# Two queries' attends side by side on TensorE, and the eight PSUM banks shared out anew for the query stage

## The chip, the cores and the metric

One core of one Trainium2 chip runs the whole program. The metric is the device time of one execution in microseconds (us). Of several runs the median is given; a profile comes from one execution, and its span leaves out what lies ahead of the first and behind the last instruction.

Engines are named as the profile names them: PE is TensorE's matmul side and PEld its weight load, DVE is VectorE, ACT is ScalarE, POOL is GpSimd, SP is SyncE, which here issues transfers and loads registers. PSUM is the memory that PE writes to; it has eight banks of 128 partitions by 512 fp32 values.

## The reference, cut to what matters

```python
q, k, v = split(x @ wqkv)                       # 2048 tokens, 16 heads of 28
phi_q = concat(softmax(q @ w_phi), softmax(-(q @ w_phi)))     # 56 features a head; phi_k likewise
num = phi_q @ (phi_k^T @ v)                     # linear attention, per head
den = phi_q @ sum(phi_k) + 1e-6
a = (num / den) @ wo
# top 2 of 8 experts for each token, gated
b = sum over the two experts e of w_e * (silu(x @ w1[e]) @ w2[e])
out = sigmoid(x . gate_w) * a + (1 - that) * b
```

The change touches only the query side of the attention: phi_q, num, den and the product with wo.

## The kernel before, in words

The 2048 tokens are 16 tiles of 128; t counts them. The kernel runs in three stages, one after the other on PE: first values and keys of all tiles, then the queries, then the experts. The order of PE, ACT, DVE and (around the query stage) POOL is the order in which the code is written: each engine does its instructions in turn, and a wait holds up all that stands behind it on that engine.

The query stage is the loop `for t in range(NT + 2)` (L1175). For one query tile the work goes through these steps, which lie in different passes of the loop:

- `ask(t)` (L635): eleven products `pq<-WHq,WLq` on PE into one bank of tag A. `signs` (L573) copies them and their negative into an `eq` buffer on ACT, `tops` (L579) takes maxima on DVE, `drop` (L584) subtracts them on POOL (`eq<-eq,mxq`, L586), `raise_` (L644) takes the exponential on ACT (L645).
- `flip(t)` (L706): eight transposes `et<-ident,eq` on PE in two halves of four, each half into a bank of tag O, each copied out by ACT (L713). It is called two passes ahead of the attend.
- `attend(t)` (L880): 32 matmuls `n<-B,et` with 64 by 64 tiles of the array into a pair of banks of tag T. The trace shows two records for each.
- `weigh(t, n_)` (L888): six DVE instructions that read `n` (L895 to L901), then two on POOL that make `om` (L906, L908).
- `turn(t)` (L910), one pass later: four transposes `ot<-ident,om` into a bank of tag O, and `xsplit` (L136), a copy on ACT (`oh<-ot`, L137) and two subtractions on DVE (L139, L140), which read that bank last.
- `project(t)` (L918), one pass later still: eleven products `ao` into tag A, left by ACT in `leave_row` (L923) and written out by SP.

One pass of the loop thus holds, on PE in this order: attend(t), flip(t+2), project(t-2), turn(t-1), ask(t+7), and in the late passes the transposes `xgt` of `first_tokens` (L851), a turn of gathered rows for the experts, into tag O and read by ACT (L824) and DVE (L828, L829). On POOL: up to three stores `tabd<-rec` of `store` (L473), which wait for the matmul in `behind`, here the attend of the pass; then `drop`, then `om`. In pass 0 or 1 `route` (L397) lets PE count the experts' tokens into a bank `pp` of tag O, which DVE reads at L458, behind `xsplit` of query 0.

The banks are shared out once for the whole program: two for A (L91, `BANKS`), four for O, one pair for T (L94). A tile of a tag gets a bank when the last reader of the tile that held it is done.

The functions that the diff touches, and what calls them:

Of the kernel before, what the change touches and what calls it, by code (L numbers as in the profile page):

```python
# [8 lines left out]
F32 = mybir.dt.float32  # L9
# [6 lines left out]
PSUM = bass.MemoryType.PSUM  # L16
DRAM = bass.MemoryType.DRAM

P = 128
# [6 lines left out]
NT = S // P  # L26
# [25 lines left out]
QASKS = {t: t + 7 for t in range(9)}  # L52
# [10 lines left out]
LANDING = ("x00", "w0", "x10", "x20", "x30", "w1", "x01", "x40", "x11", "x50", "x21", "w2", "x31", "w3", "x41", "x51")  # L63
PIECES = ("00", "10", "20", "30", "01", "40", "11", "50", "21", "02", "12", "22", "31", "41", "03", "13", "23",
          "32", "51", "42", "52", "33", "43", "53")
BANKS = {"A": 2, "O": 4}
XLP = range(3, 16)
QBUFS = 5
ASKS = {9: 0, 10: 1, 11: 2, 12: 3, 14: 4}
# [2 lines left out]
NJ = 8  # L72
# [10 lines left out]
def gated_mix(ctx: ExitStack, tc: tile.TileContext, xt, xq, wk, wq, wv, wphi, wo, w12, out):  # L83
# [3 lines left out]
    cst = ctx.enter_context(tc.tile_pool(name="cst", bufs=1))  # L87
    dram = ctx.enter_context(tc.tile_pool(name="dram", bufs=1, space=DRAM))
    ps = ctx.enter_context(tc.tile_pool(name="ps", bufs=1, space=PSUM))

    def bank(tag, name):  # L91
        return ps.tile([P, 512], F32, tag=tag, name=name, bufs=BANKS[tag])

    def two_banks(name):  # L94
        return ps.tile([P, NJ, P], F32, tag="T", name=name, bufs=1)

    def after(i, others):
        for o in others:
# [21 lines left out]
    reached = {}  # L120
# [15 lines left out]
    def xsplit(xh, xl, src, eng):  # L136
        nc.scalar.activation(xh, src, AF.Copy)  # L137
        lo = xh[64:P, 3]
        for i in (eng.tensor_tensor(out=lo, in0=src[64:P, 3], in1=lo.bitcast(F32), op=ALU.subtract),  # L139
                  eng.tensor_tensor(out=xl, in0=src[:, 0:3], in1=xh[:, 0:3].bitcast(F32), op=ALU.subtract)):  # L140
            if eng is nc.gpsimd:
                in_turn(i)
# [21 lines left out]
    pe = pe_stack.enter_context(tc.tile_pool(name="pe", bufs=1, side="right"))  # L164
# [63 lines left out]
    for what in LANDING:  # L228
        t = int(what[1])
# [41 lines left out]
    for t in range(NT):  # L271
        pool = pe if t < NT // 2 else px
# [3 lines left out]
    for n, m in (("k", D), ("v", VG), ("q", D), ("o", D)):  # L276
        pool = px if n in "qo" else pb
# [75 lines left out]
    for what in LANDING:  # L353
        t = int(what[1])
# [3 lines left out]
        c = FIRST[int(what[2])]  # L358
# [114 lines left out]
    def store(n, behind=()):  # L473
        for at, what in stores[:n]:
            i = in_turn(nc.gpsimd.indirect_dma_start(
                out=tabd[:, :], out_offset=bass.IndirectOffsetOnAxis(ap=at, axis=0), in_=what, in_offset=None), "slots")
            after(i, [*filled, *behind])
            for o in sc:
                tc.declare_no_dep(i.ins, o.ins, reason="slots of their own")
            sc.append(i)  # L480
        del stores[:n]
# [91 lines left out]
    def signs(e, src):  # L573
        e4 = signed(e)
        nc.scalar.activation(e4[:, :, 0], src, AF.Copy)
        nc.scalar.activation(e4[:, :, 1], src, AF.Copy, scale=-1.0)


    def tops(e, n, pool):  # L579
        mx = pool.tile([P, H, 2], F32, tag="mx", name=f"mx{n}", bufs=2)  # L580
        nc.vector.tensor_reduce(out=mx, in_=signed(e), axis=AX.X, op=ALU.max)
        return mx

    def drop(e, mx):  # L584
        e4 = signed(e)
        in_turn(nc.gpsimd.tensor_tensor(out=e4, in0=e4, in1=mx.unsqueeze(3).to_broadcast([P, H, 2, DH]),  # L586
                                        op=ALU.subtract))

    def lower(e, n, pool):
        drop(e, tops(e, n, pool))  # L590
# [36 lines left out]
    def advance(n):  # L627
        for _ in range(n):
            if routes and next(routes[0], 0) == 0:
                del routes[0]  # L630
# [13 lines left out]
    def raise_(t):  # L644
        nc.scalar.activation(EQ[t][:, :, 0:56], EQ[t][:, :, 0:56], AF.Exp)  # L645
# [19 lines left out]
    for t in range(NT):  # L665
# [19 lines left out]
        if 1 <= t < 5:  # L685
            c = t - 1
# [193 lines left out]
    def attend(t):  # L880
        n_ = two_banks(f"n{t}").rearrange("p (a j) (b d) -> p a (j b) d", a=2, b=2)
        for j in range(NJ):
            for a, h in enumerate(half):
                for b in half:
                    reached["n"] = nc.tensor.matmul(n_[b, a, j, 0:60], et[t][h, j, b], B[h, j], start=True, stop=True)
        return n_.rearrange("p a j d -> p (a j) d")
# [20 lines left out]
                                        in0=w5[:, :, :, 0], in1=w5[:, :, :, 1], op=ALU.add))  # L907
        in_turn(nc.gpsimd.tensor_copy(o[:, D:512], o[:, 384:D]))  # L908

    def turn(t):  # L910
        oh[t] = pc.tile([P, 4, P], F32R, tag="oh", name=f"oh{t}")
        ol[t] = pc.tile([P, 3, P], F32R, tag="ol", name=f"ol{t}")
        tp = bank("O", f"ot{t}").rearrange("p (c n) -> p c n", n=P)
        for c in range(4):
            nc.tensor.transpose(tp[:, c], om[t][:, c * P:(c + 1) * P], ident)
        xsplit(oh[t], ol[t], tp, nc.vector)
# [11 lines left out]
    def table():  # L928
        for r in range(E):
            v = nc.values_load(byrank[0:1, r:r + 1], engines=SPONLY, min_val=0, max_val=E - 1)  # L930
            todo = [(tabm[:, r * nm:(r + 1) * nm], tabd[bass.ds(v * OWN, MAIN), :], P)]
            if r < LARGE:
                n = extra(r)
                for h in range(copies(r)):
                    todo.append((tabx[h * n:(h + 1) * n, r:r + 1], tabd[bass.ds(v * OWN + MAIN, n), :], n))
            for dst, src, p in todo:
                i = nc.sync.dma_start(dst, src.rearrange("(c p) two -> p c two", p=p))
                after(i, sc)

    def rows(lo, hi):  # L940
        in_turn(nc.gpsimd.tensor_scalar(idm[:, lo * nm:hi * nm], tabm.bitcast(I32)[:, lo * nm:hi * nm, 0], float(S - 1), None,
                                op0=ALU.min))
        if lo < LARGE:
            hi = min(hi, LARGE)
            in_turn(nc.gpsimd.tensor_scalar(idx[:, lo:hi], tabx.bitcast(I32)[0:EX, lo:hi, 0], float(S - 1), None, op0=ALU.min))
# [218 lines left out]
    def fill_in():  # L1164
        n = len(fill)
        fill.append((*FILL[n // 2], n % 2))
        first(*fill[-1])

    def part_way():
        for g in list(coming):  # L1170
            if next(g, 0) == 0:
                coming.remove(g)

    at, k = None, 0
    for t in range(NT + 2):  # L1175
        u = t + QAHEAD
        if t - 1 in QASKS:
            signs(EQ[QASKS[t - 1]], pq[QASKS[t - 1]])
        elif t == 0:
            signs(EQ[6], pq[6])  # L1180
        if 1 <= t and u - 1 < NT:
            raise_(u - 1)
        advance(QSTEPS.get(t, 2))
        early_top = u < NT and t < LOWER
        if early_top:
            top = tops(EQ[u], f"q{u}", pr)
        if at is not None and t == at + 1:
            store(LASTS, behind)
            table()
        if t < NT:  # L1190
            n_ = attend(t)
        behind = [reached["n"]]
        store(STORES.get(t, 3) if at is None or at == NT else 0, behind)
        if at is None and not routes:
            routes.append(ranks())
            at = NT
        if at == NT and len(stores) <= LASTS and not routes:
            at = t
        k = t - (NT if at is None else at)
        if k == ROWS + 1:  # L1200
            rows(0, 1)
        for c in ASKED.get(k - ROWS, ()):
            gather(0, c, behind)
        if early_top:
            drop(EQ[u], top)
        if t < NT:
            weigh(t, n_)
        if u < NT and not early_top:
            lower(EQ[u], f"q{u}", pr)
        if t + 2 < NT:  # L1210
            flip(t + 2)
        if t >= 2:
            if t == NT + 1:
                fill_in()
            leave_row(t - 2, project(t - 2))
        if t == NT:
            fill_in()
        if 1 <= t <= NT:
            turn(t - 1)
        if t in QASKS:  # L1220
            ask(QASKS[t], some=(0 if t else 5, 11))
        if t == NT - 1:
            fill_in()
        if t == PEND:
            pe_stack.close()
            pm = ctx.enter_context(tc.tile_pool(name="pm", bufs=2, side="right", reuse_waits="tile"))
            pw = ctx.enter_context(tc.tile_pool(name="pw", bufs=1, side="right", reuse_waits="tile"))
            ph = ctx.enter_context(tc.tile_pool(name="ph", bufs=2, side="right", reuse_waits="tile"))
        if k == ROWS + 3:
            rows(1, E)  # L1230
        if k == 2:
            load(0)
            splits += [halve(0, 1), halve(0, 2)]
        part_way()
        if ROWS + 2 <= k < ROWS + 3 + nm:
            g = first_tokens(k - ROWS - 2)
            next(g)
            coming.append(g)
        if SPLIT <= t < SPLIT + 3 and splits:
            if next(splits[0], 0) == 0:  # L1240
                del splits[0]
                if splits:
                    next(splits[0])
    assert not coming and not splits
    runs["on"] = False
    pc_stack.close()
    px_stack.close()
# [14 lines left out]
    for s in range(E * NFC):  # L1262
# [28 lines left out]
        n = 3 * nm  # L1291
        if e == E - 1 and fc > NFC - LATE:
            n = n // 2 if fc < NFC - 1 else 0
        if fc % 2 == 0:
            f = first_pair(e, fc // 2)
# [7 lines left out]
    with tc.manual_schedule(engines={mybir.EngineType.PE}):  # L1303
        last = reached["pe"]
        for cs in ((0, 1), (2,), (3,)):
            for at in (0, 2):
                for c in cs:
                    for i in range(2):
                        share(E - 1, NFC - LATE + at + i, c, last)
                    if at:  # L1310
                        leave(E - 1, (c,))
    pf_stack.close()


    loads, (n_ov,) = nc.values_load_multi_w_load_instructions(nov_i[0:1, 0:1], min_val=0, max_val=MAXOV)  # L1315
# [98 lines left out]
```

## Time and profile before

| what | value |
|---|---|
| median of 3 runs | 790.08 us (789.95 to 791.45) |
| the profiled execution's own time | 790.2 us |
| its span | 788.2 us |
| PE busy | 777.1 us, 99% of the span |
| DVE, ACT, POOL busy | 483.4, 308.9, 339.9 us |
| granted TensorE clock, mean | 0.998 |

The profiled execution lies 0.1 us above the median, and 2.0 us of its time lie outside the span. A row of the timeline gives the start, the time from the first start to the last end of the records that it merges, the engine, the line, the operation with what it writes and reads, how many records, and in brackets how long the engine sat idle before and what released it. Matmuls overlap: one that is listed with 0.37 us lets the next start after about 0.20 us, so differences of starts tell what PE spends on a group.

### The profile page before, as it was taken

The page shows a single profiled execution, that of the slowest core. Times are in us where ns is not written, and L with a number is a line of the kernel's source. Part 1 is how long each engine was busy: PE and PEld are TensorE (multiplying, and loading weights), DVE is VectorE, ACT ScalarE, POOL GpSimd, SP SyncE. Part 2 cuts the span into 40 slices and gives each one's busy share as a digit, 9 for nine tenths or more (in the row PEclk, how much of TensorE's full clock was granted, in tenths as well). Part 3 has the DMA queues.
Part 4 walks back from the last instruction along what each step waited for, and adds up shares of the span by engine and source line. Part 5 has one row for each costly group of instructions (what it writes and reads, how often), then busy time and mean ns, then how long its engine had stood idle before and what let it go on. Part 6 is the DMA issues. An engine that isn't in the chain of part 4 may idle for free. (4 is left out here: it accounts for less than half of the span.)

```text
span 788.2 us, 18163 instructions
## 1 busy us (share of the span) xinstructions
PE 777.1 (99%) x7378; PEld 721.4 (92%) x7378; DVE 483.4 (61%) x1045; ACT 308.9 (39%) x523; POOL 339.9 (43%) x334
## 2 busy tenths in 40 slices
PE   8999999999999999999999999999999999999996
PEld 6888888989999999998999799999999999999995
DVE  4698978658684866574566345554754555475431
ACT  5543455556532433343334223333433333243221
POOL 4667878886223316423450147144325405423003
PEclk9999999999999999999999999999999999999999
DMA  8420000135253337324543264364345336435403
GB/s 280 121 86 1 2 2 26 38 54 180 98 170 90 111 105 164 127 94 97 144 139 109 63 144 147 112 154 130 123 120 153 129 125 157 137 129 115 134 2 46
DMA packets 39786, 85.92 MB, mean 109 GB/s; under 512 B 11312, under 2 KB 20928, under 8 KB 39700
## 3 DMA queue, kind: packets, MB, share of 16 engines
q1 hardware_dynamic: 29332, 67.88, 26.3%
q0 software_dynamic: 10224, 16.61, 11.3%
q8 instruction: 59, 0.97, 0.5%
q10 hardware_dynamic: 144, 0.23, 0.1%
q14 instruction: 27, 0.22, 0.1%
HBM read 71.89 MB, written 12.82 MB: 107 GB/s over the span
## 5 line engine op out<-in xcount | busy, mean ns | idle before, releaser
L1088 PE MATMUL acc<-w2h,hx 64*128 64x448 f32 (+2 forms) x1088 | 193.1, 363 | 0.1
L1037 ACT ACTIVATE hs<-hp 128x272 f32<-128x272 f32 (+4 forms) x154 | 70.8, 483 | 306.5 <-issue 185.8
L804 POOL DMA_INDIRECT xg<-in_xq_dram,idq x114 | 126.2, 1107 | 148.7 <-PE hp L125 52.3
L1043 DVE CAST hx<-hs 128x504 fp32r<-128x504 f32 (+5 forms) x154 | 55.5, 361 | 204.1 <-ACT hs L1037 204.0
L1088 PEld LDWEIGHTS acc<-w2h,hx 64*128 64x128 f32 (+2 forms) x1088 | 161.3, 182 | 4.9 <-ACT y L1141 1.6
L1088 PE MATMUL acc<-w2l,hx 64*128 64x448 f32 (+3 forms) x544 | 157.9, 363 | 0.0
L1004 PE MATMUL hp<-xgh,w1h 64*128 64x504 f32 (+2 forms) x490 | 149.3, 386 | 0.0
L1004 PE MATMUL hp<-xgh,w1l 64*128 64x504 f32 (+2 forms) x490 | 149.1, 385 | 0.0
L1004 PE MATMUL hp<-xgl,w1h 64*128 64x504 f32 (+2 forms) x490 | 148.8, 384 | 0.0
L960 POOL DMA_INDIRECT out_dram<-y,tabm x32 | 52.4, 1637 | 172.2 <-DVE y L1143 163.7
L1122 PE MATMUL acc<-w2h,hx 128*128 128x448 f32 (+2 forms) x366 | 111.6, 365 | 0.0
L1088 PEld LDWEIGHTS acc<-w2l,hx 64*128 64x128 f32 (+3 forms) x544 | 96.9, 182 | 1.4
L1004 PEld LDWEIGHTS hp<-xgh,w1h 64*128 64x128 f32 x490 | 87.9, 184 | 3.3 <-issue 0.3
L1004 PEld LDWEIGHTS hp<-xgh,w1l 64*128 64x128 f32 x490 | 88.1, 185 | 3.0
L1004 PEld LDWEIGHTS hp<-xgl,w1h 64*128 64x128 f32 x490 | 88.0, 184 | 3.0
L1046 DVE TENSOR_TENSOR hx<-hs,hx 128x276 fp32r<-128x276 f32 (+5 forms) x168 | 84.9, 512 | 5.3
L125 PE MATMUL hp<-xgh,w1h 128*128 128x272 f32 (+1 forms) x336 | 87.8, 289 | 0.0
L125 PE MATMUL hp<-xgh,w1l 128*128 128x272 f32 (+1 forms) x336 | 87.7, 289 | 0.0
L773 DVE TENSOR_TENSOR w1l<-wr,w1h 128x1024 fp32r<-128x1024 f32 x56 | 68.2, 1218 | 11.0 <-ACT w1h L771 10.0
L1122 PEld LDWEIGHTS acc<-w2h,hx 128*128 128x128 f32 (+2 forms) x366 | 68.0, 186 | 6.2 <-issue 0.7
L1122 PE MATMUL acc<-w2l,hx 128*128 128x448 f32 (+2 forms) x190 | 69.4, 365 | 0.0
L125 PEld LDWEIGHTS hp<-xgh,w1h 128*128 128x128 f32 x336 | 63.3, 188 | 0.6
(231 smaller groups left out, 1415.1 us busy)
## 6 DMA issues: line engine op xcount, KB each, us to landing
wr<-in_w_dram SPq DMA_DIRECT2D x56, 512.0 KB, 3.6
wr<-in_w_dram SPq DMA_DIRECT2D x46, 448.0 KB, 4.4
kept<-in_w_dram SPq DMA_DIRECT2D x10, 448.0 KB, 4.3
out_dram<-aos SPq DMA_DIRECT2D x16, 224.0 KB, 3.9
xr<-in_xt_dram SPq DMA_DIRECT2D x10, 256.0 KB, 4.5
xg<-in_xq_dram,idq POOLq DMA_INDIRECT x114, 2.7
xr<-in_xt_dram SPq DMA_DIRECT2D x6, 192.0 KB, 4.2
out_dram<-zero SPq DMA_DIRECT2D x5, 224.0 KB, 5.2
```

The costliest lines, as they stand in the source:

```text
L125: reached["pe"] = nc.tensor.matmul(o, a, b, start=i == 0, stop=i == n - 1)
L773: nc.vector.tensor_tensor(out=l, in0=raws[s][layer - 1], in1=h.bitcast(F32), op=ALU.subtract)
L804: i = nc.gpsimd.indirect_dma_start(out=t[:, b], out_offset=None, in_=xq, in_offset=bass.IndirectOffsetOnAxis(ap=idq[:, e, 4 * c + b:4 * c ...
L960: return nc.gpsimd.indirect_dma_start(out=out, out_offset=bass.IndirectOffsetOnAxis(ap=idx_ap, axis=0), in_=y, in_offset=None, compute_op= ...
L1004: meet(("first", i), a, lambda: nc.tensor.matmul(o[i], l, r, start=n == 0, stop=n == len(rounds) - 1), n == 0)
L1037: nc.scalar.activation(hs[:, tsl], hp, AF.Silu)
L1043: nc.vector.tensor_copy(h[:, tsl], hs[:, tsl])
L1046: nc.vector.tensor_tensor(out=h[:, a + o:b + o], in0=hs[:, a:b], in1=h[:, a:b].bitcast(F32), op=ALU.subtract)
L1088: meet((e, c), a, lambda: nc.tensor.matmul(acc[e][c][:l.shape[1], 0:D], l[half[a]], r[half[a]], start=new, stop=ends and c not in of[k + 1 ...
L1122: i = nc.tensor.matmul(acc[e][c][:l.shape[1], 0:D], l, r, start=fc == 0 and k == 0, stop=fc == NFC - 1 and k == len(pr) - 1)
```

## The change

It gives the query stage pools of its own. For its length, T has two pairs of banks, O two banks, A two as before; afterwards O has four and T one pair again. In an even pass attend(t) and attend(t+1) stand behind one another on PE; an odd pass has none. The stores of an even pass wait for the second attend, those of an odd pass for the last product of the pass before. `turn` takes a bank of tag A in passes 9 to 13, when nothing is asked any more, and of tag O otherwise.

```diff
-BANKS = {"A": 2, "O": 4}
+BANKS = {"T": 1, "O": 4}
+IN_PAIRS = {"T": 2, "O": 2}
...
+    banks = {"A": (ps, 2)}
+
+    def share_out(name, bufs):
+        if "stack" in banks:
+            banks["stack"].close()
+        banks["stack"] = ExitStack()
+        pool = banks["stack"].enter_context(tc.tile_pool(name=name, bufs=1, space=PSUM, reuse_waits="tile"))
+        banks.update({tag: (pool, n) for tag, n in bufs.items()})
...
+    share_out("ps0", BANKS)
...
-    def turn(t):
+    def turn(t, tag="O"):
...
-        tp = bank("O", f"ot{t}").rearrange("p (c n) -> p c n", n=P)
+        tp = bank(tag, f"ot{t}").rearrange("p (c n) -> p c n", n=P)
...
+    share_out("ps1", IN_PAIRS)
     at, k = None, 0
+    asked_of = {}
     for t in range(NT + 2):
...
         if t < NT:
-            n_ = attend(t)
-        behind = [reached["n"]]
+            if t % 2 == 0:
+                for a in range(2):
+                    asked_of[t + a] = attend(t + a)
+            n_ = asked_of[t]
+            behind = [reached["n" if t % 2 == 0 else "pe"]]
+        else:
+            behind = [reached["n"]]
...
-            turn(t - 1)
+            turn(t - 1, "O" if t in QASKS or t + 2 >= NT else "A")
...
     assert not coming and not splits
+    share_out("ps2", BANKS)
```

What it does to the order on PE, at three places. The instructions of ACT, DVE and POOL keep their order; on SP one write of a finished row moves behind five register loads. In the rows below a name in brackets is an engine for whose semaphore the instruction waits (Activation is ACT), and the lines of the change are 3 to 13 higher than before.

Pass 1 on PE, around the transposes of query 3 and of query 0's result (`om`). Before:

```order
L454 MATMUL pp_1720<-selb_1182,ones_b 128x8
L885 MATMUL n_1732<-B,et_1550 64x60 [waits DVE_49,PE_49]
L885 MATMUL n_1732<-B,et_1550 64x60 x31
L712 MATMUL et_1779<-ident,eq_205 128x128 [waits Activation_49]
L712 MATMUL et_1779<-ident,eq_205 128x128 x3
L712 MATMUL et_1785<-ident,eq_205 128x128 [waits Activation_49]
L712 MATMUL et_1785<-ident,eq_205 128x128 x3
L915 MATMUL ot_1793<-ident,om_1685 128x128 [waits Activation_49,Pool_49]
```

and in the change:

```order
L467 MATMUL pp_1760<-selb_1185,ones_b 128x8
L725 MATMUL et_1786<-ident,eq_208 128x128 [waits Activation_49,Pool_49]
L725 MATMUL et_1786<-ident,eq_208 128x128 x3
L725 MATMUL et_1792<-ident,eq_208 128x128 [waits Activation_49]
L725 MATMUL et_1792<-ident,eq_208 128x128 x3
L928 MATMUL ot_1800<-ident,om_1725 128x128 [waits Activation_49,Pool_49]
```

Attend 1 has gone from here to pass 0, behind attend 0; the two halves of query 3's transposes and `ot` now follow `pp` directly.

Pass 2 on PE, the change: the first pair in the steady part of the stage, with the last products of pass 1 ahead of it.

```order
L655 MATMUL pq_1808<-WHq,XL_178 128x448 x3
L898 MATMUL n_1838<-B,et_1728 64x60 [waits DVE_49]
L898 MATMUL n_1838<-B,et_1728 64x60 x31
L898 MATMUL n_1871<-B,et_1785 64x60 [waits DVE_49]
L898 MATMUL n_1871<-B,et_1785 64x60 x31
L725 MATMUL et_1921<-ident,eq_210 128x128 [waits DVE_49,Activation_49]
```

Before, `n_1831` stood here alone, between products and transposes, and `n_1944` at the same place one pass later.

The turn from pass 10 to 11 on PE, where the gathered rows' transposes stand ahead of query 13's. Before:

```order
L860 MATMUL xgt_2865<-ident,x_2774 128x128 [waits PE_49,Pool_49]
L860 MATMUL xgt_2865<-ident,x_2774 128x128 x3
L885 MATMUL n_2878<-B,et_2736 64x60 [waits DVE_49,PE_49]
L885 MATMUL n_2878<-B,et_2736 64x60 x31
L712 MATMUL et_2927<-ident,eq_205 128x128 [waits Activation_49]
L712 MATMUL et_2927<-ident,eq_205 128x128 x3
L712 MATMUL et_2933<-ident,eq_205 128x128 [waits Activation_49]
```

and in the change:

```order
L873 MATMUL xgt_2905<-ident,x_2781 128x128 [waits Activation_49,Pool_49]
L873 MATMUL xgt_2905<-ident,x_2781 128x128 x3
L725 MATMUL et_2934<-ident,eq_208 128x128 [waits Activation_49]
L725 MATMUL et_2934<-ident,eq_208 128x128 x3
L725 MATMUL et_2940<-ident,eq_208 128x128 [waits DVE_49,Activation_49]
```

The attend between the two groups of transposes is gone, and the second half of query 13's transposes has a wait for DVE that it had not. Between passes 12 and 13 the same rows follow each other for query 15, there with a wait for ACT alone on both halves.

## Rows read from the trace of the kernel before

**Rows 1.** The page: the span, PE's share of it, and the granted clock in 40 slices of the span (tenths of full speed, 9 is 90% or more).

```profile
span 788.2 us, 18163 instructions
...
PE 777.1 (99%) x7378; PEld 721.4 (92%) x7378; DVE 483.4 (61%) x1045; ACT 308.9 (39%) x523; POOL 339.9 (43%) x334
...
PEclk9999999999999999999999999999999999999999
```

**Rows 2.** Busy time by stretch, the expert stage: the stretch, its length, then each engine's busy time with its instructions (PE, PEld, DVE, ACT, POOL), the granted clock, the share of the DMA engines and GB/s.

```profile
222.00:500.00 278.00, 278.00 (x2010) 263.11 (x2010) 171.03 (x427) 98.64 (x167) 105.99 (x88) 1.00 0.43 122
500.00:780.00 280.00, 279.93 (x2565) 266.44 (x2562) 143.50 (x243) 92.65 (x134) 86.10 (x67) 1.00 0.42 118
```

**Rows 3.** What PE waited for between 100 and 230 us: who waited for whom, us in total, times, the longest.

```profile
PE n L885 <- DVE w L901: 1.0, 2, 0.6
PE ot L915 <- POOL om L906: 0.2, 1, 0.2
```

**Rows 4.** PE's timeline in passes 0 to 2, cut to the groups that the argument uses.

```profile
117.70 1.16 PE L885 MATMUL n<-B,et 64*64 64x60 f32 x64 [0.62 <-DVE w L901]
...
120.04 0.66 PE L915 MATMUL ot<-ident,om 128*128 128x128 f32 x4 [0.16 <-POOL om L906]
...
121.98 0.37 PE L642 MATMUL pq<-WLq,XH 128*128 128x448 f32 x1
122.19 0.78 PE L642 MATMUL pq<-WHq,XL 128*128 128x448 f32 x3
122.89 1.16 PE L885 MATMUL n<-B,et 64*64 64x60 f32 x64
123.98 1.09 PE L712 MATMUL et<-ident,eq 128*128 128x128 f32 x8
124.83 0.45 PE L125 MATMUL ao<-WHo,oh 128*128 128x448 f32 x1
...
127.15 0.60 PE L915 MATMUL ot<-ident,om 128*128 128x128 f32 x4
127.51 0.45 PE L642 MATMUL pq<-WHq,XH 128*128 128x448 f32 x1
```

**Rows 5.** The attend's matmuls as a group: durations in ns (least, median, most), first and last start.

```profile
L885 PE MATMUL n<-B,et x1024: 218/218/264, 113.5 to 203.5; 64*64 64x60 f32 x171
```

**Rows 6.** The attend's matmuls that were under way in the first 0.10 us of attend 2: the stretch, its length, PE's busy time with the number of records, clock, DMA.

```profile
122.89:122.99 0.10, 0.10 (x4) 1.00 0.00 0
```

**Rows 7.** POOL's timeline in passes 0 and 1.

```profile
114.92 0.97 POOL L475 DMA_INDIRECT tabd<-rec,slot_i  x1 [1.50 <-PE n L885]
...
117.18 1.71 POOL L586 TENSOR_TENSOR eq<-eq,mxq 128x896 f32<-128x896 f32 x1
```

**Rows 8.** ACT's timeline in pass 1.

```profile
118.93 0.95 ACT L645 ACTIVATE eq<-eq 128x896 f32<-128x896 f32 x1 [1.06 <-POOL eq L586]
119.79 1.06 ACT L713 ACTIVATE et<-et 128x512 f32<-128x512 f32 x2
120.74 0.60 ACT L137 ACTIVATE oh<-ot 128x512 fp32r<-128x512 f32 x1
```

**Rows 9.** DVE's timeline in pass 1: the last reader of query 0's `ot`, and behind it the reader of `pp`.

```profile
121.81 0.56 DVE L140 TENSOR_TENSOR ol<-ot,oh 128x384 fp32r<-128x384 f32 x1
122.28 0.22 DVE L458 TENSOR_TENSOR pos<-pp,base 128x72 f32<-128x72 f32 x1
```

**Rows 10.** PE's timeline in passes 6, 10, 12 and 14: `ot` of query 6, the gathered rows' transposes, `ot` of query 13, and the last attend.

```profile
162.29 0.60 PE L915 MATMUL ot<-ident,om 128*128 128x128 f32 x4
...
181.59 0.60 PE L860 MATMUL xgt<-ident,x 128*128 128x128 f32 x4
...
192.04 0.60 PE L860 MATMUL xgt<-ident,x 128*128 128x128 f32 x4
...
201.23 0.60 PE L915 MATMUL ot<-ident,om 128*128 128x128 f32 x4
201.75 0.44 PE L860 MATMUL xgt<-ident,x 40*128 40x40 f32 x4
202.55 1.16 PE L885 MATMUL n<-B,et 64*64 64x60 f32 x64 [0.36 <-DVE w L901]
```

**Rows 11.** DVE's timeline in pass 10: the last reader of the gathered rows' bank.

```profile
183.73 0.56 DVE L829 TENSOR_TENSOR xgl<-xgt,xgh 128x384 fp32r<-128x384 f32 x1
```

**Rows 12.** ACT's timeline in passes 12 to 14: the copies out of the gathered rows' bank and of query 13's `ot`.

```profile
192.81 0.61 ACT L824 ACTIVATE xgh<-xgt 128x512 fp32r<-128x512 f32 x1
...
201.96 0.59 ACT L137 ACTIVATE oh<-ot 128x512 fp32r<-128x512 f32 x1
```

**Rows 13.** POOL's timeline: the first store of pass 2 and of pass 4, and the last instruction for query 6.

```profile
125.21 1.00 POOL L475 DMA_INDIRECT tabd<-rec,slot_i  x1 [1.86 <-PE et L712]
...
139.53 0.99 POOL L475 DMA_INDIRECT tabd<-rec,slot_i  x1 [0.48 <-PE et L712]
...
160.31 0.24 POOL L908 COPY om<-om 128x64 f32<-128x64 f32 x1
```

**Rows 14.** PE's last matmul in the timeline of the end.

```profile
780.16 0.36 PE L1122 MATMUL acc<-w2h,hx 128*104 128x448 f32 x1
```

**Rows 15.** Busy time by stretch behind it; columns as in the second group, the granted clock is the third number from the end.

```profile
782.00:784.00 2.00, 0.00 (x0) 0.00 (x0) 0.00 (x0) 0.00 (x0) 1.12 (x1) 1.00 0.83 115
784.00:786.00 2.00, 0.00 (x0) 0.00 (x0) 0.00 (x0) 0.00 (x0) 0.00 (x0) 0.93 0.57 83
```

More of the change, by code (lines that the diff above doesn't have):

```diff
@@ L89, in gated_mix @@
     ps = ctx.enter_context(tc.tile_pool(name="ps", bufs=1, space=PSUM))
+    banks = {"A": (ps, 2)}
[5 more added lines that the diff above has]
+        banks.update({tag: (pool, n) for tag, n in bufs.items()})
     def bank(tag, name):
-        return ps.tile([P, 512], F32, tag=tag, name=name, bufs=BANKS[tag])
+        pool, n = banks[tag]
+        return pool.tile([P, 512], F32, tag=tag, name=name, bufs=n)
     def two_banks(name):
-        return ps.tile([P, NJ, P], F32, tag="T", name=name, bufs=1)
+        pool, n = banks["T"]
+        return pool.tile([P, NJ, P], F32, tag="T", name=name, bufs=n)
+    share_out("ps0", BANKS)
     def after(i, others):
@@ L1312, in gated_mix @@
     pf_stack.close()
+    ctx.push(banks["stack"])
     loads, (n_ov,) = nc.values_load_multi_w_load_instructions(nov_i[0:1, 0:1], min_val=0, max_val=MAXOV)
```

## The prediction

> **What bounds the kernel now.** First the page: PE is busy for 99% of the span, at full clock in every slice [rows 1]. Then the windows: behind the query stage PE is idle for less than 0.1 us in 558 [rows 2]. So whatever moves the end of the query stage by some time moves the end of the run by the same time. Last, PE's waits: in the whole query stage they are 1.2 us, before two attends for `weigh`'s last read of `n` and once for `om` [rows 3]. ACT, DVE and POOL are off the path as long as PE doesn't wait for them. So the change is priced by two sums: what PE's own instructions get shorter, and which waits appear on PE.
>
> **What a pair saves.** Look at attend 2 [rows 4]. The last three products ahead of it start at 122.19. One product alone is listed at 0.37, the three together at 0.78, so the third starts 0.41 after the first and each takes a slot of 0.205. The slots end at 122.19 + 0.615 = 122.80; the attend starts at 122.89, 0.09 late, and the first `et` starts at 123.98. A lone attend thus takes 1.18 us. The eight `et` behind it take 0.85 to the `ao` at 124.83, while four `ot` take 0.36 (127.15 to 127.51) and eight should take about 0.80; I add 0.05 and have 1.23. What is an attend's own pace? Its 64 records end at 122.89 + 1.16 = 124.05, each lasts 0.218 [rows 5], and four had begun in the first 0.10 us [rows 6]. The other 60, fifteen groups of four, thus begin between 122.99 and 124.05 - 0.218 = 123.83, in 0.84 us: 0.056 a group, and about 0.058 with some room for rounding, so 16 groups take 0.93. The second attend of a pair costs that, since the array is already cut into 64 by 64 tiles and the way in and out is paid once: 1.23 - 0.93 = **0.30 us a pair**. Bounds: 0.18, when only a gap of 0.09 goes on either side, and 0.36. Eight pairs save 2.4 (1.4 to 2.9). Attend work is otherwise the same; no matmul is added or removed.
>
> Against this stands the Trainium skill, "TensorE: Matmul & The Clock Gate", Part 2, "Back-to-back issue gap": it gives matmuls of at most 64 columns an issue floor of about 25 ns. By the page an attend would need 64 x 25 ns = 1.6 us in whatever company it stands (an estimate), pairs would save nothing, and the sum below would be about +6.0. The measured attend begins 64 records in less than 1.0 us, four side by side, so the trace decides against it.
>
> **The old waits go.** The second attend of a pair has a pair of T banks of its own, so the two waits for `weigh` have no reason left, and `om0` is asked for later: -1.2.
>
> **The price: two O banks instead of four.** A transpose now waits for the reader of the tile two before it. Four places, each against the time at which PE would want the bank.
>
> *Pass 1.* PE came to attend 1 at 117.70 - 0.62 = 117.08; that work is now in pass 0 and costs 0.93 there, so PE reaches `et3` at 118.01. `pp` holds one O bank until DVE reads it, and that read stands behind DVE's last one of `ot0` in DVE's order. Both halves of `et3` and then `ot0` must therefore go through the other bank, one after the other. The second half is wanted half of 0.85 later, at 118.44, but waits for ACT's copy of the first. On ACT that copy stands behind `raise_(4)`, which waits for POOL's `drop(4)`, which stands behind two stores; and the stores began 1.50 us after waiting for attend 0 [rows 7], and now wait for attend 1 behind it, 0.93 later. So `raise_` moves from 118.93 to 119.86, and the copy from 119.79 to 120.72 [rows 8]. One copy is half of the 1.06 row: done at about 121.3, and the second half starts at 121.34. **Wait 2.9.** It ends 0.43 later, at 121.77, where `ot0` wants the same bank; ACT takes 0.70 from such a start to the copy's start (`ot` 120.04 to `oh` 120.74) and 0.55 for the copy: 122.65. **Wait 0.9.** Behind the waiting transposes stand `ot0`, pass 1's products and the first steady pair, and ACT, DVE and POOL get all these later too. Then `pp` itself is read behind `ot0`'s last reader, as before within 0.5 us [rows 9], and the bank is free when pass 2 wants it.
>
> *Pass 11.* The gathered rows' `xgt` hold one bank from 181.59 [rows 10] until DVE's last read ends at 183.73 + 0.56 = 184.29 [rows 11], 2.70 later. Without the attend in between, the second half of `et13` wants it after 0.43 + 0.43 = 0.86. **Wait 1.8.**
>
> *Pass 13.* The same, but here the second half of `et15` waits for ACT's copy of the first half, which stands behind `xgh`: from `xgt` at 192.04 to 192.81 + 0.61 = 193.42 are 1.38, and 0.55 for the copy makes 1.93 [rows 12]. **Wait 1.1.**
>
> *Pass 15.* `ao13` reads `oh`, which ACT finishes at 201.96 + 0.59 = 202.55, 1.32 after `ot13` started [rows 10, 12]. PE came to attend 15, which covered this, at 202.55 - 0.36 = 202.19, 0.96 after `ot13`; without it, 0.8 to 0.96 after. **Wait 0.5** (0.36 at least).
>
> In the other passes two halves of `et` and one `ot` share two banks with products of 2 us or more between them, and ACT's copies follow within 1.3 us: no wait. The four `turn`s in tag A use banks that nobody has asked for since a pass.
>
> **Edits that cost nothing.** The sharing out has no instruction of its own; the first tiles of either new pool wait for readers that finished earlier in the passes shown. SP's write of a finished row is moved behind five register loads; its buffer is one of three, wanted again three passes later, some 21 us. The later gate of even stores costs POOL nothing at first: POOL is the one queue that could run out of time. Its stores begin 7.16 us apart a pass (125.21 to 139.53 for two), more than PE's 7.03, and `om6` is done at 160.31 + 0.24, 1.74 before `ot6` starts [rows 13]. In the change POOL loses 2.7 at pass 1 and PE only 1.7 by pass 6 (savings of three pairs), which leaves 0.7. If that is used up, PE waits for `om` by up to 1 us in the last passes. I take 0 and keep +1 for the range.
>
> **The sum.** New waits 2.9 + 0.9 + 1.8 + 1.1 + 0.5 = 7.2; saved 2.4 and 1.2: **+3.6 us**. The profiled execution took 790.2, so 793.8; it lies 0.1 above the median, so **793.7**. Bounds of this case: the late readers at passes 11 to 15 can gain 0.5 of their delay back once PE waits for them (0.5 less), and savings of 2.9 instead of 2.4, make +2.6; savings of 1.4 and a POOL wait of 1 make +5.6: 792.7 to 795.7. All of it is above 0.2% (1.6 us), which is about what a measurement can tell from no change.
>
> **Rivals.**
> *Neutral.* The long wait at pass 1 rests on one bank being blocked by `pp`. If the read of `pp` came ahead of the second half of `et3`, the two halves would not be tied, and `ot0` alone would wait about 1.1 for `om0` and its bank. Then 3.8 becomes 1.1, and the sum +0.9: 791.0 (790.2 to 791.6). Against it stands DVE's order, in which `pp` comes 0.47 behind the start of `ot0`'s last reader. Chance 0.11.
>
> *Faster.* The evacuation keeps ahead of PE: at passes 1, 11 and 13 ACT and DVE, whose busy shares are 39% and 61% [rows 1], empty a bank by the time PE is back. Price: only -2.4 - 1.2, or 786.6. It decides from the point where the new waits are under 3.6, half of what the rows give; pass 1 alone gives 3.8 by the order of instructions, not by a lack of speed. Chance 0.05.
>
> *Slower by the clock.* PE has not stood still for 2.9 us anywhere in the stage. If the clock fell to the lower of its two levels, 1.2 GHz, the eleven products behind would cost 11 x 0.205 = 2.3 more, a whole pass 7: 796 to 801. Against it: PE's last matmul ends at 780.16 + 0.36 [rows 14] and the clock is still 1.00 up to 784, to fall only after that [rows 15]. The Trainium skill, "TensorE: Matmul & The Clock Gate", Part 1, has the array go to 1.2 GHz when it is idle for long enough; by that rule this rival is a matter of the wait's length, and no run here shows a stop of this length. Chance 0.04.
>
> **How the numbers follow.** Forecast 0.80, rivals 0.11, 0.05 and 0.04. Slower by over 0.2% are the forecast and the clock, 0.84; within it the neutral case, 0.11; faster 0.05. The forecast's own range reaches from 792.7 to 795.7; to hold 8 in 10 with something left for a bound I have mis-sized, I stretch it downwards into the neutral case, to 790.7.
>
> **What would show it.** In the profile after: PE waits of about 7 us in all between 113 and 215; at pass 1 one of 2.9 before `et`, released by ACT, and one of 0.9 before `ot`; at pass 11 about 1.8 before `et` by DVE; at 13 about 1.1 by ACT; at 15 about 0.5 before `ao`; pairs of 128 records in about 2.1 us (1.16 + 0.93); none of the old waits for `w`; clock 1.00. The forecast is wrong if the 128 records take 1.9 or less, if `et` at pass 1 waits less than 2, or if POOL's `om` appears as a releaser in the last passes.

## The result: 0.8 to 1.2% slower, twice the forecast

The changed kernel takes 798.07 us (median of 6, 796.29 to 800.16), the kernel before 790.14 beside it (6 runs): ratio 1.0099, 95% interval 1.0082 to 1.0116, or +7.9 us. The forecast was 793.7 with a range of 790.7 to 795.7: right in sign, too small by 4.4 us. The profiled execution took 798.34 us.

The page of the changed kernel, with the lines that answer to [rows 1]:

```profile
span 796.4 us, 18154 instructions
...
PE 779.1 (98%) x7378; PEld 725.5 (91%) x7378; DVE 481.6 (60%) x1045; ACT 309.9 (39%) x523; POOL 339.4 (43%) x334
...
PEclk9999998999999999999999999999999999999999
```

Read the last line first: there is an 8 in the seventh slice, about 119 to 139 us, where before there were only nines. PE has the same 7378 matmuls and is busy for 2.0 us longer, so some of them ran slower.

PE's waits between 100 and 215 us, as in [rows 3]:

```profile
PE et L725 <- ACT et L726: 3.7, 2, 2.8
PE et L725 <- DVE xgl L842: 1.8, 1, 1.8
PE ot L928 <- ACT et L726: 0.8, 1, 0.8
PE ao L138 <- ACT oh L150: 0.4, 1, 0.4
PE n L898 <- issue: 0.3, 1, 0.3
```

The first four are the forecast's new waits, with the releasers that it named: 2.8 and 0.8 at pass 1, 1.8 at pass 11, 3.7 - 2.8 = 0.9 at pass 13, 0.4 at pass 15. The last has no releaser (`issue`: PE waited for nothing that the profile shows) and was not forecast.

PE's timeline, passes 0 to 2, against [rows 4]:

```profile
114.04 2.09 PE L898 MATMUL n<-B,et 64*64 64x60 f32 x128
116.06 1.09 PE L725 MATMUL et<-ident,eq 128*128 128x128 f32 x8
...
118.46 0.64 PE L725 MATMUL et<-ident,eq 128*128 128x128 f32 x4
121.94 1.11 PE L725 MATMUL et<-ident,eq 128*128 128x128 f32 x4 [2.84 <-ACT et L726]
123.83 1.09 PE L928 MATMUL ot<-ident,om 128*128 128x128 f32 x4 [0.78 <-ACT et L726]
...
127.33 0.57 PE L655 MATMUL pq<-WLq,XH 128*128 128x448 f32 x1
...
128.47 2.09 PE L898 MATMUL n<-B,et 64*64 64x60 f32 x128
```

Four transposes last 0.64 us before the wait and 1.11 behind it; a product 0.57 us, where it was 0.37 [rows 4]. The windows name the cause (the clock is the third number from the end, as in [rows 15]):

```profile
116.00:120.00 4.00, 3.10 (x38) 2.53 (x27) 3.62 (x10) 2.06 (x4) 3.23 (x3) 1.00 0.03 5
120.00:124.00 4.00, 1.28 (x5) 0.91 (x6) 1.51 (x3) 2.03 (x3) 3.94 (x5) 0.63 0.00 0
124.00:128.00 4.00, 4.00 (x14) 3.63 (x14) 2.19 (x10) 0.60 (x1) 0.79 (x2) 0.52 0.00 0
128.00:132.00 4.00, 4.00 (x142) 3.61 (x141) 3.21 (x8) 2.57 (x5) 1.00 (x1) 1.00 0.01 4
```

A clock of 0.50 is 1.2 GHz, the lower of the two levels; 0.63 over the second window means that it fell near 121.0, 1.9 us after PE's last matmul had ended (118.46 + 0.64). By the third window, 0.52, it was back at full speed only near 127.8, after transposes and products from 123.83 on. So in this trace a wait for a bank has a second price. The Trainium skill, "TensorE: Matmul & The Clock Gate", Part 1, has an array that was idle run at 1.2 GHz until work releases it; this trace agrees, with a fall near 121.0 and a return near 127.8.

The chain ahead of the wait, on ACT, against [rows 8]:

```profile
120.45 0.95 ACT L658 ACTIVATE eq<-eq 128x896 f32<-128x896 f32 x1 [1.07 <-POOL eq L599]
121.31 0.58 ACT L726 ACTIVATE et<-et 128x512 f32<-128x512 f32 x1
```

With this execution's attends starting 0.59 later (114.04 against 113.45), the exponential comes 120.45 - 118.93 - 0.59 = 0.93 later, exactly the second attend, as forecast.

To place the loss, two rows more of the kernel before, the first attend and the first product of the expert stage:

```profile
113.45 1.16 PE L885 MATMUL n<-B,et 64*64 64x60 f32 x64
...
206.33 0.38 PE L125 MATMUL hp<-xgh,w1h 128*128 128x276 f32 x1
```

and of the changed kernel the latter with PE's last matmul:

```profile
213.81 0.37 PE L138 MATMUL hp<-xgh,w1h 128*128 128x276 f32 x1
...
787.88 0.36 PE L1135 MATMUL acc<-w2h,hx 128*104 128x448 f32 x1
```

| stretch | before | after | difference |
|---|---|---|---|
| start to the first attend | 113.45 | 114.04 | +0.59 |
| first attend to first `hp` (the stage) | 92.88 | 99.77 | +6.89 |
| first `hp` to PE's last matmul [rows 14] | 573.83 | 574.07 | +0.24 |
| behind it, in the span | 8.04 | 8.52 | +0.48 |
| outside the span | 2.0 | 1.9 | -0.1 |

The stage is what the change touches; ahead of it the two kernels do the same work, and over all the profiles below the first attend starts anywhere from 113.05 to 115.02.

### The profile page after: what moved, and what is told of

The parts are those of the page before. It is cut to its first block, busy times and chain, and to the rows that moved or that the text cites. A ratio compares the mean times of both kernels' runs of the same rounds, so it can differ in the third digit from the quotient of the medians.

```text
span 796.4 us, 18154 instructions
## 1 busy us (share of the span) xinstructions
PE 779.1 (98%) x7378; PEld 725.5 (91%) x7378; DVE 481.6 (60%) x1045; ACT 309.9 (39%) x523; POOL 339.4 (43%) x334
```

## The experiments

Three numbers are read from each trace: first attend to attend 2 (pass 1 lies in it), first attend to first `hp` (the stage), and whether the clock falls in the stage. From c5_rotate on the runs were made on chips where the kernel before itself takes 795.8 to 796.1 instead of 790.1; there the trace of every kernel has a stretch of clock at 0.50 at about 490 to 505 us, in the expert stage, and from the first `hp` to the last matmul it takes 578.9 to 580.9 instead of 573.8 to 574.1. No trace of the kernel before was taken there. So across chips only the ratios compare, and the stretches ahead of that place.

| run | median, before beside it | ratio (95%) | to attend 2 | stage | clock falls in the stage |
|---|---|---|---|---|---|
| before | | | 9.44 | 92.88 | no |
| the change | 798.07, 790.14 | 1.0099 (1.0082 to 1.0116) | 14.43 | 99.77 | yes |
| c1_warm | 796.07, 790.09 | 1.0069 (1.0056 to 1.0082) | 12.17 | 97.09 | no |
| c2_gate | 794.31, 790.09 | 1.0056 (1.0042 to 1.0071) | 11.20 | 95.83 | no |
| c3_from2 | 791.64, 790.09 | 1.0021 (1.0012 to 1.0029) | 9.42 | 94.50 | no |
| c4_banks | 794.51, 790.09 | 1.0049 (1.0037 to 1.0061) | 12.78 | 98.03 | yes |
| c5_rotate | 798.31, 795.85 | 1.0026 (1.0014 to 1.0037) | 9.43 | 93.61 | no |
| c6_two_to_nine | 796.45, 795.85 | 1.0000 (0.9991 to 1.0010) | 9.42 | 93.22 | no |
| c7_pp_in_a | 801.99, 795.85 | 1.0063 (1.0044 to 1.0081) | 12.35 | 98.78 | yes |
| c8_again | 803.74, 795.82 | 1.0105 (1.0087 to 1.0124) | 13.71 | 99.86 | yes |
| c9_two_to_nine | 796.15, 795.82 | 1.0006 (0.9997 to 1.0016) | 9.44 | 93.21 | no |
| c10_odd | 798.28, 795.82 | 1.0031 (1.0019 to 1.0044) | 9.42 | 95.27 | no |
| c11_after | 803.55, 796.11 | 1.0097 (1.0079 to 1.0114) | 14.48 | 100.72 | yes |
| c12_warm | 802.81, 796.11 | 1.0081 (1.0066 to 1.0096) | 12.17 | 98.49 | no |

**The clock: the wait filled with products.** c1_warm:

```diff
             tp = bank("O", f"et{t}{a}")
+            if a and spare is not None:
+                for k in range(14):
+                    nc.tensor.matmul(spare[:, 0:D], XH[0][:, 0], WH["q"][:, 0], start=True, stop=True)
...
+        spare = bank("A", f"pq{QASKS[1]}") if t == 1 else None
...
-            flip(t + 2)
+            flip(t + 2, spare)
...
-            ask(QASKS[t], some=(0 if t else 5, 11))
+            ask(QASKS[t], spare, some=(0 if t else 5, 11))
```

> The changed kernel with fourteen products more (128x448, 14 x 0.205 = 2.9 us), put between the two halves of query 3's transposes, into the bank that the next products will start anew. They fill the wait of 2.84 us at pass 1 and add nothing behind it. Theory (clock): the waits and savings are as forecast, +3.6, and the rest of the loss is the clock, which the trace of the changed kernel shows at 0.50 from about 121 to 128 us and which costs 2.4 us there by the starts of ot0 (+3.2 instead of +2.6) and of attend 2 (+5.0 instead of +2.6). Then the clock stays at 1.00 here and the time is 793.7 to 795.5, at least 2 us below the changed kernel. Rival (the waits cost more than their rows, or the stage loses elsewhere): time as the changed kernel, 797 to 798.5, the lost time simply carried by the products.

PE's timeline in pass 1, then the window of its second half:

```profile
118.96 0.64 PE L728 MATMUL et<-ident,eq 128*128 128x128 f32 x4
119.35 3.08 PE L726 MATMUL pq<-WHq,XH 128*128 128x448 f32 x14
122.44 0.66 PE L728 MATMUL et<-ident,eq 128*128 128x128 f32 x4
123.88 0.63 PE L931 MATMUL ot<-ident,om 128*128 128x128 f32 x4 [0.78 <-ACT et L729]
```

```profile
122.00:126.00 4.00, 3.21 (x20) 2.48 (x19) 0.89 (x4) 1.58 (x3) 3.26 (x5) 1.00 0.00 0
```

The transposes come no earlier, but last 0.66 instead of 1.11, and the clock stays at 1.00. First attend to attend 2 is 2.26 shorter, the median 2.0 lower. The median still missed its range by 0.6: its trace has a start 1.08 later than before's. The same pair side by side:

> The changed kernel once more, on one chip with the next, so that the price of the clock at pass 1 is the difference of the two. Theory (clock): the trace has a stretch at 0.50 that begins while PE waits in pass 1; from the first attend to attend 2 13.7 to 14.5 us.

> The changed kernel with the fourteen products in the wait of pass 1, as c1_warm. Theory (clock): no stretch at 0.50 before the expert stage, from the first attend to attend 2 12.2 us, and 1.5 to 2.7 us less than c11_after; the rest of the loss (waits and pauses) stays: 4.5 to 6 over the kernel before. Rival (the difference between c1_warm and the changed kernel was one of chips): within 0.8 us of c11_after.

From 14.48 to 12.17, 2.31 us, and the stage 2.23 shorter, as expected; the stretch at 0.50 is gone (c11_after, then c12_warm):

```profile
124.00:128.00 4.00, 4.00 (x26) 3.11 (x28) 3.34 (x11) 0.43 (x2) 0.00 (x0) 0.50 0.00 0
```

```profile
124.00:128.00 4.00, 4.00 (x140) 3.53 (x139) 3.75 (x13) 1.82 (x3) 0.28 (x2) 1.00 0.01 4
```

The medians differ by 0.74 only, under the 1.5 that was expected and inside the rival's 0.8. In the two profiles the expert stage took 1.65 longer in c12_warm (580.89 against 579.24), at a place that no kernel here changed: PE is idle there for part of the time in both, and the clock behind it averages 0.61 and 0.70 over 495 to 505 us, where c11_after has 1.00 and 0.66. The price of 2.3 us is thus read from the traces; the medians alone would leave it between 0.7 and 2.0. The mean clock of each execution points to a fall in all of the changed kernel's, and not in the profiled one alone: 0.990 to 0.991 in the six of c11_after, 0.993 to 0.996 in the six of c12_warm, 0.992 to 0.996 in those of the kernel before beside them.

**The chain: the gate of the stores.** c2_gate:

```diff
                 for a in range(2):
                     asked_of[t + a] = attend(t + a)
+                    if a == 0:
+                        behind = [reached["n"]]
+            else:
+                behind = [reached["pe"]]
             n_ = asked_of[t]
-            behind = [reached["n" if t % 2 == 0 else "pe"]]
```

> The changed kernel, but the stores of an even pass wait for the first attend of the pair. The chain at pass 1 (stores, drop, raise_, copy) then starts 0.93 earlier: the wait before the second half of et3 falls from 2.84 to about 1.9, the one before ot0 stays at 0.8 or less. Theory (clock): -0.9 for sure; if a stop of 1.9 us leaves the clock at 1.00, -0.9 - 2.4, about 794.7; if it still falls, 797.1. Rival (the chain does not hang on the gate): wait 2.84 and time 798 as before the edit.

```profile
120.53 0.66 PE L725 MATMUL et<-ident,eq 128*128 128x128 f32 x4 [1.88 <-ACT et L726]
121.97 0.63 PE L928 MATMUL ot<-ident,om 128*128 128x128 f32 x4 [0.78 <-ACT et L726]
```

The wait is 2.84 - 1.88 = 0.96 shorter, the clock held in this execution, and the median is 794.31 for the 794.7 that was expected. Its six runs spread from 793.51 to 796.02. That the clock falls in some of them and not in others would fit, but there is a trace of one only.

**Pairs from pass 2 on.** c3_from2, which keeps passes 0 and 1 as they were:

```diff
-    share_out("ps1", IN_PAIRS)
...
-            if t % 2 == 0:
+            if t < 2:
+                asked_of[t] = attend(t)
+            elif t % 2 == 0:
+                if t == 2:
+                    share_out("ps1", IN_PAIRS)
...
-            behind = [reached["n" if t % 2 == 0 else "pe"]]
+            behind = [reached["n" if t < 2 or t % 2 == 0 else "pe"]]
```

> The changed kernel, but the first two passes are as in the kernel before (single attends, four O banks, one pair for T); the banks are shared out and the pairs begin at pass 2. Theory: no wait at pass 1 but the old ones (0.62 and 0.16), so no fall of the clock; seven pairs save 7 x 0.29 = 2.0; the waits at passes 11, 13 and 15 stay (1.8 + 0.9 + 0.4), the old 0.36 goes: +0.7, 790.8. Rival (pairs themselves cost PE time, as the stop of 0.7 us inside one pair at 158 us of the changed kernel's trace hints): 0.7 per stop more, 791.5 to 794.

6.4 us of the 7.9 go with the first two passes. Pass 1 is as before (9.42), the later waits are the change's (1.8, 0.9, 0.4). The fourth pair of the change has 0.42 us too much here: the rival's pause, though smaller.

**The banks alone.** c4_banks has single attends (`n_ = attend(t)`, `behind = [reached["n"]]`) in the change's banks.

> Only the banks of the change (two pairs for T, two for O) with single attends in their old places. Theory: pass 1 waits still, since pp holds one O bank and both halves of et3 and ot0 go through the other: et3 at 118.2, its second half when the copy behind raise_ is done, about 120.4 instead of 118.6, wait 1.6; ot0 about 0.7; passes 11 and 13, where the attend now covers 0.93, 0.9 and 0.2; old waits gone: +2.4, 792.5, clock 1.00 if a stop of 1.6 leaves it there. Rival (the tie of the banks needs the pairs): within 0.5 us of the kernel before.

```profile
121.97 0.66 PE L725 MATMUL et<-ident,eq 128*128 128x128 f32 x4 [1.66 <-ACT et L726]
123.41 1.09 PE L928 MATMUL ot<-ident,om 128*128 128x128 f32 x4 [0.78 <-ACT et L726]
```

The waits are there without any pair, as expected (1.6 and 0.7 were given); the clock fell all the same in this execution (`ot` lasts 1.09), the slowest of the six at 796.62. The median of 794.51 is over the 792.5 that was expected; besides the clock, the later waits are larger than given, three of 0.55 in passes 11 to 13 instead of 0.9 and 0.2. So with waits of 1.66 and 0.78 the clock fell here, and with 1.88 and 0.78 it did not in c2_gate: in these traces the length of a wait doesn't settle it.

**The tie by `pp`.** c7_pp_in_a takes `bank("A" if banks["T"][1] == 2 else "O", f"pp{r}")` for the counts.

> The changed kernel, but the routing counts pp go to a bank of tag A, so that the two halves of et3 have a bank each. Theory: the halves are no longer tied to each other, but ot0 still waits for the copy of et3's first half behind raise_, and for om0, which are late by the gate: about 1.3 us later than in the kernel before instead of 3.2; one wait of some 2.3 before ot0 in place of 2.84 and 0.78. With the later waits (+1.2) that is +2.5, 792.6, if the clock holds, up to 795 if it falls. Rival (pp is not what ties them): waits and time as the changed kernel, 798.

```profile
118.02 1.07 PE L725 MATMUL et<-ident,eq 128*128 128x128 f32 x8
121.58 1.09 PE L928 MATMUL ot<-ident,om 128*128 128x128 f32 x4 [2.50 <-ACT et L726]
```

All eight transposes run at once, so `pp` was the tie; `ot0` comes 7.99 after the first attend, 1.40 later than before (1.3 was given), after one wait of 2.50. The clock falls again, and two pairs pause for 0.35 and 1.47 (2.44 and 3.56 us long), so that the loss is 6.1 where 2.5 to 4.9 was expected. Untying alone is not enough.

**Four banks in turn at the end.** c5_rotate is c3_from2 with

```diff
     def bank(tag, name):
+        if name[0:2] in ("et", "ot", "ao", "xg") and "turns" in banks:
+            banks["turns"] += 1
+            tag = "AAOO"[banks["turns"] % 4]
...
+            if t == 10:
+                banks["turns"] = -1
...
+            banks.pop("turns", None)
```

> Pairs from pass 2 as in c3_from2, and in passes 10 to 15 the tiles of transposes, products with wo and gathered rows go round all four single banks (A, A, O, O and again) in PE's order, so that each waits for the tile four before it and not two. Theory: in c3_from2 PE stopped at passes 11 and 13 only because two O banks were too few; both waits (start to start 2.06 and 1.15 instead of 0.09) vanish, -3.0 against its 791.6: 788.6, 1.5 under the kernel before, unless a stop inside a pair (0 to 0.7 in the traces so far) adds to it. Rival: other readers come next, ao9 and ao11 waiting for oh as ao13 does (0.4 to 0.6 each): 789.5 to 790.

```profile
PE ao L141 <- ACT hs L1053: 1.1, 1, 1.1
PE n L901 <- issue: 1.1, 2, 0.6
PE ao L141 <- ACT et L729: 0.5, 1, 0.5
PE ao L141 <- DVE ol L156: 0.5, 1, 0.5
PE ao L141 <- ACT oh L153: 0.4, 1, 0.4
```

A miss: slower than before, not 1.5 faster. The waits of `et` are gone, but others come: `ao` waits 0.5 each in passes 11 and 13, the places that the rival named, though the releasers listed are DVE's `ol` and ACT's `et` and not `oh`. Its new turn also let a later `ao` meet a bank of the experts (1.1, behind the stage). Of the 1.1 listed for `issue`, 0.62 is the old wait ahead of attend 1; the rest belongs to a pause inside a pair, and two pairs last 2.39 and 3.05 instead of 2.09, 1.3 together.

**Pairs where no wait comes.** c6_two_to_nine and c9_two_to_nine: c3_from2, with single attends and the old banks again from pass 10 on (`if t == 10: share_out("ps2", BANKS)`).

> Pairs at passes 2, 4, 6 and 8 alone, in the banks of the change; passes 0, 1 and from 10 on as in the kernel before, with its banks. Theory: no new wait anywhere; four pairs save 4 x 0.29 = 1.2: 788.9, or up to 0.7 more with a stop inside the fourth pair. Rival (pairing saves less than n-to-n distances of 13.77 against 14.06 say): 790.1.

> Pairs at passes 2, 4, 6 and 8 alone, as in c6_two_to_nine, whose trace had pauses of 0.6 and 1.0 us inside pairs with no releaser. Theory: without pauses 1.2 under the kernel before; with the pause at instruction 3860 to 3880 alone (0.3 to 0.6) 0.6 to 0.9 under. Rival (pauses eat all of it): no difference.

No wait is left but the old ones, and nothing is won: ratios 1.0000 and 1.0006. PE's rows of its third pair and, behind the last pair, of the lone attend of pass 10 tell why:

```profile
151.97 2.09 PE L898 MATMUL n<-B,et 64*64 64x60 f32 x120
154.25 0.40 PE L898 MATMUL n<-B,et 64*64 64x60 f32 x8 [0.20 <-issue]
...
177.83 1.06 PE L898 MATMUL n<-B,et 64*64 64x60 f32 x38
179.29 0.65 PE L898 MATMUL n<-B,et 64*64 64x60 f32 x26 [0.39 <-issue]
```

The pair lasts 2.69 instead of 2.09 (154.25 + 0.40 - 151.97, rounded), and the lone attend 2.11 instead of 1.16. Without the two the stage would be 93.22 - 0.60 - 0.95 = 91.67; four pairs at 0.29 forecast 92.88 - 1.16 = 91.72. So pairs do save 0.29 each, and pauses take it back. (Whether the kernel before pauses at pass 10 on this chip too is not known; its trace is from another, and shows none.)

**Pauses.** In the changed kernel the fourth pair:

```profile
156.00 1.96 PE L898 MATMUL n<-B,et 64*64 64x60 f32 x114
158.30 0.50 PE L898 MATMUL n<-B,et 64*64 64x60 f32 x14 [0.34 <-issue]
```

From 157 to 160 us the DMA queues moved three packets, all of them code (packets, MB, share of the engines):

```profile
q14 instruction: 2, 0.02, 4.5%
q8 instruction: 1, 0.02, 4.4%
```

The pause comes at instruction 3866 of PE (weight loads, matmuls and the semaphore and branch steps that the trace lists between them), and a load of 16 KB on queue 8 starts within 0.1 us of it, at 157.79. In c3_from2, c6_two_to_nine and c7_pp_in_a the pair's pause comes at 3870, 3878 and 3874, and in c1_warm, where 28 instructions more stand ahead, at 3862, some 30 earlier within the pair. A place in the code, then, and not a step of the work? c8_again and c10_odd asked that:

> The changed kernel once more, beside the two that follow and the kernel before. Theory (clock at pass 1, waits, and PE stops for code inside pairs): about 8 us slower than the kernel before; in the trace a stretch at clock 0.50 behind pass 1 and, where PE pauses inside a pair with no releaser, the pause lies at the same count of PE instructions as before (3860 to 3880 from the first), which is instruction 224 to 240 of the fourth pair's 256. Rival (the loss is a matter of that one chip): less than 5.

> Pairs at passes 3, 5 and 7 (queries 3 to 8), all else as in the kernel before. The third pair then spans PE instructions 3841 to 4097 from the first. Theory (a pause belongs to a place in the code, and comes where PE has run through the code ahead of it faster than it is fetched): instruction 3866 now has slow products ahead of it, so no pause there; 3 x 0.29 = 0.9 under the kernel before, stage 92.0 us. Rival (the pause belongs to pairs as such): 0.3 to 0.7 less gain, a pause near the end of a pair.

c8_again pauses at 3874, as expected, and confirms the +7.9. Its clock falls later than in the changed kernel's first trace, near 123.5, when PE is already busy with products behind the waits of 2.85 and 0.78:

```profile
123.00:124.00 1.00, 1.00 (x7) 0.91 (x6) 0.06 (x1) 0.60 (x1) 0.94 (x2) 0.75 0.00 0
124.00:126.00 2.00, 2.00 (x7) 1.78 (x6) 1.85 (x8) 0.00 (x0) 0.13 (x1) 0.50 0.00 0
```

First attend to attend 2 is 13.71 there, 1.5 over c12_warm's 12.17: the same wait cost 1.5 in one execution and 2.3 in two others.

c10_odd (pairs at passes 3, 5, 7 by `elif t % 2`, old banks from pass 9) has none at 3866, but one of 0.9 in its second pair, at 3684 to 3691, and there too a load on queue 8 is just starting. So a fixed count was wrong; what stays is that pauses come inside attends, pairs above all, where PE runs 256 instructions in 2 us, and that at the first such place of a run a load of code starts within 0.4 us of it. That a load causes them is not shown, and some rows speak against it: PE runs again at 158.30 while the load of 157.79 takes 2.12 us, and in c7_pp_in_a and c12_warm the load starts at 155.54 and 155.05, when PE already runs again (155.50 and 154.96). A load at 130.35 starts inside the changed kernel's second pair, which does not pause, no kernel moved a load alone, and at the place in pass 10 (4477 to 4493 in most of the later runs, in a pair or in a lone attend) no load is listed. The cause of the pauses stays open. The rest of c10_odd's miss (stage 95.27 for 92.0) is `ao` waiting 1.0 for `oh` and an attend 1.0 for `w` behind the last pair; why DVE and ACT are late there was not tried.

## Why the prediction was wrong, step by step

- **What a pair saves** held: attend to attend over two passes is 13.77 (128.47 to 142.24 in the changed kernel, 2.09 for 128 records) against 2 x 7.03; 0.29 for 0.30. The issue floor of 25 ns in the Trainium skill ("TensorE: Matmul & The Clock Gate", Part 2, "Back-to-back issue gap") was rightly set aside: 128 records start within 2.09 - 0.22 = 1.87 us, 15 ns each.
- **The new waits** held one by one: 2.84, 0.78, 1.8, 0.9, 0.4, 6.7 in sum for 7.2. An idle time costs a little more than it shows, since the overlap with the matmul ahead is lost too: at pass 11 two transposes start 2.06 apart instead of 0.11, 1.95 for a wait of 1.8. In c2_gate, without fall or pause, the stage is 95.83 - 92.88 = 2.95 longer; with the 0.93 that its gate gives back, 3.9 for the forecast's 3.6. c1_warm, also without a fall, agrees: 4.21 longer, less a pause of 0.30.
- **The clock** is the step that failed: the sum let PE stand for 2.9 us at pass 1 and run on at 1.00, where the runs show a fall that costs 2.3. The rival was named and its price bounded (2.3 for eleven products; 2.3 measured), but it got a chance of 0.04 on one row: the clock had stayed at 1.00 for over 3 us behind the last matmul [rows 14, 15]. One fall was taken for a rule. Here it came 1.9 us after the last matmul, and with two of the shorter stops as well (c4_banks, c7_pp_in_a).
- **"Attend work is otherwise the same"** missed the pause: 0.7 in the fourth pair (2.79 for 2.09). No row of before could show it, since there no 256 such instructions stand together. It is the second term that the sum lacked, and its cause is open; without the clock alone the range would still have been missed, for c1_warm takes 796.07.
- **The sum**: 3.9 + 2.3 + 0.7 = 6.9, the 6.89 of the stage. The other 1.2 of the profiled run lie where both kernels do the same: start 0.59, behind the last matmul 0.48, expert stage 0.24. The starts of the other profiles scatter by more than that, so no run here shows whether the change has a part in it.
- **The neutral rival** had the right tie but too small a price: with `pp` out of the way (c7_pp_in_a) `ot0` alone waits 2.50, not 1.1.
- POOL's backlog, kept for the range, did not show: no wait for `om`.

## What to carry to other kernels

A wait on PE is priced twice: its length, and the chance that the clock falls and everything for the next microseconds runs at half speed (1.5 to 2.3 us here); where a trace shows one fall, take its delay as one draw. Where the wait could not be removed, products of no use in it kept the clock (c1_warm, c12_warm). Count banks by who is last to read them in its engine's order: a small tile that is read late (`pp`) made two banks into one.

## What was not expected of the hardware

PE pauses without a releaser in dense runs of 64 by 64 matmuls: 0.3 to 0.7 us in the change's fourth pair (2.39 to 2.79 us long for 2.09, in most of the runs), none in the lone attends of the kernel before. And the clock did not come back with the first work behind the wait: in the changed kernel eight products in a row ran at 1.2 GHz, at 0.37 us from start to start instead of 0.205.
